# Sparse attention and MLP: x transposed by DMA for six batches, tokens taken in eight slices, outputs stored by partition halves

## The chip, the cores and the metric

The kernel runs on one core of a Trainium2 chip. The metric is the device time of one execution in microseconds (us); medians of several runs (slow ones among them) are given. For a program on one core a run counts as slow when it is over 1.5% above the fastest of the same kernel. A ratio is the mean time of one kernel's fast runs over that of the other's fast runs of the same rounds, so it is not quite the ratio of the medians quoted.

## The reference, cut to what matters

```python
B, H, S, D = 8, 8, 576, 64          # q, k, v: float32
mask_local   = (rel >= 0) & (rel < 32)                       # heads 0 to 3
mask_strided = (rel >= 0) & (pos % 32 == pos.T % 32)         # heads 4 to 7
attn = softmax(where(mask, q @ k.T / 8, -1e9)) @ v
x = attn.transpose(0, 2, 1, 3).reshape(4608, 512)            # tokens x channels
h = x @ w_in                                                 # 512 -> 2048
out = (h * tanh(softplus(h))) @ w_out                        # 2048 -> 512
```

Channels 0 to 255 of x come from the local heads, 256 to 511 from the strided heads.

## The kernel before: what the change and the argument touch

The MLP works in nine blocks of 512 tokens, numbered 0 to 8. In each block the first product fills `psh`, ScalarE applies the activation into `gT`, and the second product fills `pso`. The attention of batch t+1 is woven in between the matmuls of block t's second product. It leaves x with tokens on the partitions (`x_s[n, j]` holds token 8n+j of the strided heads), and TensorE transposes it into `xT`, a ring of four batches, with channels on the partitions:

```python
xT = const.tile([128, 4, RT], BF16, name="xT")          # RT = 4 * 576 tokens
...
def xt(self, kind, hf, eng=None):                       # kind "s": strided heads
    for j in range(CS):                                 # CS = 8
        nc.tensor.transpose(tr[:, PN*j:PN*j+PN], x_s[0:PN, j, 128*hf:128*hf+128], ident[0:PN, 0:PN])
    cast(eng, xT[:, 2 + hf, t0:t0 + S].rearrange("p (n j) -> p n j", j=CS), ...)   # ScalarE
```

The first product reads a contiguous piece of the ring, and the second product's result goes out by one large store for each 256 tokens:

```python
for a, n, o in segs(t):                                 # two pieces only where the ring ends: block 4
    for cc in (2, 3, 0, 1):
        nc.tensor.matmul(ps[:, u, o:o+n], lhsT=w_in[:, cc, ...], rhs=xT[:, cc, a:a+n], ...)
...
nc.scalar.copy(osb[:], p[:])
nc.sync.dma_start(out[r:r + 256, :].rearrange("(o p) d -> p o d", o=2), osb[:])
```

The sync engine (SP) issues its transfers in program order, each after its own wait. In block t that order is: transposes of the local q and k of batch t+1, loads of the local k and q of batch t+2, loads of v of batch t+2, the first store, transposes of the strided k and q of batch t+2, the second store. GpSimd's own queue loads the strided q and k.

The softmax here doesn't subtract the row's maximum and nothing guards it: scores larger than these inputs give would overflow.

## Time and profile before

| | before |
|---|---|
| median of 6 runs | 321.73 us (320.5 to 323.48) |
| span of the profiled run | 319.1 us |
| TensorE busy | 94% |
| a block of full attention and MLP (blocks 2, 3, 5, 6) | 32.48 us |
| TensorE's wait for `qTl` in block 1 | 1.4 us |

TensorE is the bound (94% busy), and the DMA row of the page stands at nine tenths or more for most of the first two thirds. The lines are in the prediction. A table by blocks, which the comparison will need, comes from cutting the span at the starts of the blocks' first products; the columns are the stretch, its length, the busy time of TensorE's matmuls, TensorE's weight loads, VectorE, ScalarE and GpSimd (each with its count of instructions), TensorE's granted clock as a share of full speed, the DMA share (the time of all packets over the time of the 16 engines; packets overlap, so it can pass 1) and GB/s. Of the kernel before, blocks 1 to 4:

```profile
63.83:97.88 34.05, 32.56 (x270) 16.10 (x269) 12.19 (x38) 19.80 (x23) 8.03 (x10) 1.00 1.22 199
97.88:130.36 32.48, 32.37 (x270) 16.06 (x268) 15.86 (x43) 19.75 (x22) 1.41 (x2) 1.00 1.18 202
130.36:162.84 32.48, 32.37 (x270) 16.04 (x269) 15.77 (x43) 19.74 (x22) 2.75 (x3) 1.00 1.17 175
162.84:195.48 32.64, 32.53 (x334) 22.32 (x332) 15.90 (x43) 19.75 (x22) 1.91 (x2) 1.00 1.07 168
```

Blocks 2 to 4 are full of TensorE work at full clock (granted 1.00; in block 1 TensorE waits 1.4 us), so 32.48 us is what a block costs when nothing else gets in the way.

### The profile page before, as it was taken

Reading aid. Unit: us, or ns where it says so; the run is one execution under the profiler, and the core shown is the slowest. Engines: PE = TensorE matmul, PEld = TensorE weight load, DVE = VectorE, ACT = ScalarE, POOL = GpSimd, SP = SyncE. Lnnn points to the kernel's source line nnn. Section 1 sums busy time; section 2 is a strip of 40 time slices with the busy share of each in tenths; the row PEclk is TensorE's granted clock in tenths of the full one; section 3 lists DMA queues with packets and bytes.
Section 4 is the critical chain, followed back from the end, with each engine's and each line's share of the span. In section 5 each row is a group of like instructions: output and inputs, shape, how many; then the busy total and the mean of one; then the engine's idle time right before and its main releaser. Section 6 shows DMA issues by size and latency. Waiting matters only on the chain.

```text
span 319.1 us, 5867 instructions
## 1 busy us (share of the span) xinstructions
PE 300.1 (94%) x2488; PEld 159.3 (50%) x2488; DVE 127.9 (40%) x332; ACT 172.6 (54%) x195; POOL 41.4 (13%) x50
## 2 busy tenths in 40 slices
PE   0678999999899999999999999999999999999995
PEld 0564455544454445444578555445544554444444
DVE  7672168600577047703870388028802820000000
ACT  2574563476437573767375746664666466315601
POOL 9288030145000100200020000000000000000000
PEclk9999999999999999999999999999999999999999
DMA  6999999999999999999979995898340100011011
GB/s 172 213 235 206 220 212 191 177 221 212 181 184 211 175 192 221 179 153 178 211 160 165 188 208 109 155 191 144 109 83 0 68 32 36 0 66 66 2 59 73
DMA packets 103114, 46.72 MB, mean 146 GB/s; under 512 B 85168, under 2 KB 95728, under 8 KB 103088
## 3 DMA queue, kind: packets, MB, share of 16 engines
q1 hardware_dynamic: 91648, 37.22, 64.6%
q0 software_dynamic: 11152, 8.92, 18.6%
q8 instruction: 19, 0.31, 0.4%
q10 hardware_dynamic: 288, 0.21, 0.2%
q14 instruction: 7, 0.06, 0.1%
HBM read 38.34 MB, written 9.44 MB: 150 GB/s over the span
## 4 chain that ended last, share of the span: by engine, by line
PE 81%; DVE 11%; DMA 4%; ACT 1%; issue 1%; SPq 0%; ACTq 0%
PE psh L428 38%; PE pso L467 28%; PE po L305 4%; PE pso L449 4%; DMA qTl<-ql 3%; PE ps L278 3%; DVE x_l L317 3%; DVE x_s L317 2%; PE trx L344 2%; DVE Pl L289 1%; DVE ks L151 1%; DVE rden L316 1%; DMA st<-in_k_dram 1%; PE trx L354 1%; PE tr L207 1%
## 5 line engine op out<-in xcount | busy, mean ns | idle before, releaser
L428 PE MATMUL psh<-xT,w_in 128*128 128x512 bf16 (+1 forms) x640 | 127.3, 360 | 0.0
L467 PE MATMUL pso<-w_out,gT 128*128 128x512 bf16 x512 | 126.3, 379 | 0.0
L433 ACT ACTIVATE gT<-psh 128x1024 bf16<-128x1024 f32 x72 | 73.6, 1023 | 44.0 <-PE psh L428 43.4
L428 PEld LDWEIGHTS <-w_in 128*128 128x128 bf16 x640 | 62.7, 98 | 62.2 <-issue 1.3
L467 PEld LDWEIGHTS <-gT 128*128 128x128 bf16 x512 | 43.6, 97 | 39.0
L289 DVE TENSOR_TENSOR Ps<-Ps,consts_sb 72x864 bf16<-72x864 bf16 (+1 forms) x24 | 13.2, 551 | 88.8 <-ACT Ps L283 88.8
L149 ACT COPY xT<-trx 128x576 bf16<-128x576 bf16 x32 | 20.1, 639 | 37.7 <-PE trx L354 28.2
L474 ACT COPY osb<-pso 128x1024 f32<-128x1024 f32 x16 | 16.2, 1012 | 22.6 <-PE pso L467 13.8
L283 ACT ACTIVATE Ps<-ps 72x864 bf16<-72x864 f32 (+1 forms) x24 | 18.5, 803 | 14.8 <-PE ps L278 14.8
L316 DVE RECIPROCAL rden<-po 72x4 f32<-72x4 f32 (+1 forms) x100 | 17.4, 174 | 18.8 <-PE po L305 18.6
L317 DVE TENSOR_TENSOR x_s<-po,rden 72x256 bf16<-72x256 f32 x56 | 23.5, 420 | 1.9
L151 DVE COPY osb<-pso 128x512 f32<-128x512 f32 (+1 forms) x2 | 1.1, 558 | 54.5 <-PE pso L449 54.5
L283 ACT ACTIVATE Pl<-ps 128x960 bf16<-128x960 f32 (+1 forms) x24 | 18.7, 806 | 3.6 <-PE ps L278 3.5
L305 PEld LDWEIGHTS <-Ps 72*128 72x128 bf16 x256 | 13.9, 101 | 12.5 <-DVE Ps L289 2.3
L317 DVE TENSOR_TENSOR x_l<-po,rden 96x256 bf16<-96x256 f32 x44 | 18.5, 420 | 1.5
L305 PE MATMUL po<-vs,Ps 72*128 72x65 bf16 x256 | 17.6, 201 | 0.9 <-DVE x_s L331 0.5
L97 POOL DMA_DIRECT2D ks<-in_k_dram x7 | 5.9, 842 | 80.7 <-DMA kTs<-ks 80.7
L305 PE MATMUL po<-vl,Pl 128*128 128x65 bf16 x192 | 12.9, 201 | 2.2 <-DVE x_s L317 0.7
L449 PE MATMUL pso<-w_out,gT 128*128 128x512 bf16 (+1 forms) x80 | 14.0, 336 | 0.0
L305 PEld LDWEIGHTS <-Pl 128*128 128x128 bf16 x192 | 9.9, 103 | 6.4 <-DVE x_l L317 1.8
L289 DVE TENSOR_TENSOR Pl<-Pl,consts_sb 128x960 bf16<-128x960 bf16 (+1 forms) x24 | 13.1, 545 | 0.0
L151 DVE CAST vl<-vl 128x768 bf16<-128x768 f32 x12 | 10.9, 942 | 0.8 <-DMA vl<-in_v_dram 0.8
(70 smaller groups left out, 178.0 us busy)
## 6 DMA issues: line engine op xcount, KB each, us to landing
out_dram<-osb SPq DMA_DIRECT2D x16, 512.0 KB, 3.6
vl<-in_v_dram SPq DMA_DIRECT2D x7, 768.0 KB
vs<-in_v_dram SPq DMA_DIRECT2D x8, 576.0 KB
kl<-in_k_dram SPq DMA_DIRECT2D x7, 576.0 KB, 8.7
ql<-in_q_dram SPq DMA_DIRECT2D x7, 576.0 KB, 9.4
w_out<-in_moe_w_out_dram POOLq DMA_DIRECT2D x4, 512.0 KB, 15.2
ks<-in_k_dram POOLq DMA_DIRECT2D x7, 288.0 KB, 8.0
qs<-in_q_dram POOLq DMA_DIRECT2D x7, 288.0 KB, 9.4
```

What stands on the lines that cost most here:

```text
L149: nc.scalar.copy(out_, in_)
L151: eng.tensor_copy(out_, in_)
L283: nc.scalar.activation(pt[0:n, :, 0:nw], ps[0:n, :, o0:o0 + nw], AF.Exp, scale=scale)
L289: meng.tensor_tensor(out=pm, in0=pm, in1=mk[0:n, :].unsqueeze(1).unsqueeze(1).to_broadcast([n, 2, nu, w]), op=ALU.mult,)
L305: nc.tensor.matmul(po[:, h, :], lhsT=pt[0:n, c0:c0 + 128], rhs=rhs, start=True, stop=True,)
L316: nc.vector.reciprocal(rden[0:m, :], po[0:m, :, D])
L317: nc.vector.tensor_tensor(out=dst.rearrange("p (h d) -> p h d", h=4), in0=po[0:m, :, 0:D], in1=rden[0:m, :].unsqueeze(2).to_broadcast([m, ...
L428: nc.tensor.matmul(ps[:, u, o:o + n], lhsT=w_in[:, cc, fc * 128:(fc + 1) * 128], rhs=xT[:, cc, a:a + n], start=(cc == 2), stop=(cc == 1),)
L433: nc.scalar.activation(gT[:, 2 * g:2 * g + 2, :], ps[:], AF.Mish)
L449: nc.tensor.matmul(p, lhsT=gT[:, fc, 128 * ot:128 * ot + 128], rhs=w_out[:, fc, c0:c1], start=(fc == 0), stop=(fc == 15),)
L467: nc.tensor.matmul(p[:, ot % 2, :], lhsT=gT[:, fc, 128 * ot:128 * ot + 128], rhs=w_out[:, fc, :], start=(fc == 0), stop=(fc == 15),)
L474: nc.scalar.copy(osb[:], p[:])
```

## The change

The intent is to take the strided transposes off TensorE. For batches 2 to 7 two DMA transposes per batch bring `x_s` straight into `xT_s`. A DMA transpose gives columns ordered by (j, n), so the tokens of a block are now taken as 8 slices of 64; both halves of `xT` are laid out so, with 80 columns per batch (72 used). A block crosses a batch boundary nearly always, so the first product is split in two in blocks 1 to 7. The rows of the second product come out as (parity of j, n) on the partitions, so each store becomes two DMAs of 64 partitions. The spare rows of `x_s` that the DMA transpose reads are cleared once. The local channels go first in the first product, the steps of the woven attention are reordered, and the last block's stores go mostly through ScalarE's queue in place of the sync queue.

```diff
-    xT = const.tile([128, 4, RT], BF16, name="xT")
+    xT_l = const.tile([128, 2, CS, RP], BF16, name="xT_l")
+    xT_s = const.tile([128, CS, 2, RP], BF16, name="xT_s")
...
+        def xt_dma(self, half):
+            c0, j0 = (self.b % RING) * SU, 4 * half
+            nc.sync.dma_start_transpose(
+                xT_s[:, j0:j0 + 4, :, c0:c0 + SU].rearrange("c j h n -> c (j h) n"),
+                x_s[0:SU, j0:j0 + 4, :].rearrange("p j x -> p (j x)"),
+            )
...  (steps of a batch: XD(0) after the fourth strided product, XD(1) after the eighth)
-        a, e, o, r = 512 * t, 512 * t + 512, 0, []
+        a, e, o, r = 64 * t, 64 * t + 64, 0, []
         while a < e:
-            n = min(e - a, RT - a % RT)
+            n = min(e - a, PN - a % PN)
...
+        ccs_all = (2, 3, 0, 1) if t < 2 else (0, 1, 2, 3)
...
+    def store(eng, t, ot, osb, c0=0, c1=DM):
+        rows = out[512 * t:512 * t + 512, :].rearrange("(p o i) d -> i p o d", o=4, i=2)
+        n = osb.shape[1]
+        for i in range(2):
+            eng.dma_start(rows[i, :, ot:ot + n, c0:c1], osb[64 * i:64 * i + 64])
...
+        Po.memset(x_s[64:SU], 0.0)
```

More of the change, by code (lines that the diff above doesn't have):

```diff
@@ L46 @@
     NBLK = NT // 512
-    RT = RING * S
+    RP = RING * SU
     consts_h = nc.inline_tensor(_consts(), name="consts")
@@ L338, in xt @@
             tr = tile_t("trx")[:].bitcast(BF16)
-            t0 = (self.b % RING) * S
+            c0 = (self.b % RING) * SU
             if kind == "l":
@@ L348, in xt @@
                 cast(
-                    eng, xT[:, 0:2, t0 + 288 * hf:t0 + 288 * hf + 288],
-                    tr[:, 0:576].rearrange("p (c n) -> p c n", c=2),
+                    eng, xT_l[:, :, :, c0 + 36 * hf:c0 + 36 * hf + 36],
+                    tr[:, 0:576].rearrange("p (c n j) -> p c j n", c=2, j=CS),
                 )
@@ L358, in xt @@
                 cast(
-                    eng, xT[:, 2 + hf, t0:t0 + S].rearrange("p (n j) -> p n j", j=CS),
-                    tr[:, 0:576].rearrange("p (j n) -> p n j", j=CS),
-                )
+                    eng, xT_s[:, :, hf, c0:c0 + PN],
+                    tr[:, 0:576].rearrange("p (j n) -> p j n", j=CS),
+                )
+        def xt_dma(self, half):
[4 more added lines that the diff above has]
+            )
     def attn_steps(b, x, y):
@@ L369, in attn_steps @@
         X = lambda kd, hf: (lambda: a.xt(kd, hf))
+        XD = lambda half: (lambda: a.xt_dma(half))
         s0, s1, sl2, l0, l1 = ("s", 0), ("s", 1), (("s", 2), ("l", 2)), ("l", 0), ("l", 1)
@@ L393, in attn_steps @@
             [Q(x, *sl2), Q(y, l0), V("s", 2)],
-            [V("s", 3), M("s", 2), M("l", 2)],
-            [V("s", 4), M(*l0)],
-            [Q(x, l1), V("s", 5)],
-            [V("s", 6), V("l", 5)],
-            [V("s", 7), M(*l1)],
-            [V("l", 0), V("l", 1)],
-            [X("s", 0), V("l", 2)],
-            [X("s", 1), V("l", 3)],
-            [V("l", 4), X("l", 0)],
+            [V("s", 3), XD(0), M("s", 2), V("s", 4)],
+            [V("s", 5), M("l", 2), M(*l0)],
+            [V("s", 6), V("s", 7), XD(1), Q(x, l1)],
+            [V("l", 5)],
+            [V("l", 0), M(*l1)],
+            [V("l", 1)],
+            [V("l", 2)],
+            [X("l", 0), V("l", 3)],
+            [V("l", 4)],
             [X("l", 1)], [],
@@ L407, in segs, with x_of @@
     def segs(t):
-        a, e, o, r = 512 * t, 512 * t + 512, 0, []
+        a, e, o, r = 64 * t, 64 * t + 64, 0, []
         while a < e:
-            n = min(e - a, RT - a % RT)
-            r.append((a % RT, n, o))
+            n = min(e - a, PN - a % PN)
+            r.append((a // PN % RING * SU + a % PN, n, o))
             a, o = a + n, o + n
         return r
+    def x_of(cc, a, n):
+        return xT_l[:, cc, :, a:a + n] if cc < 2 else xT_s[:, :, cc - 2, a:a + n]
     def mlp1(t, accs):
@@ L418, in mlp1, with group @@
         held = {}
-        def group(g, ccs=(2, 3, 0, 1)):
+        ccs_all = (2, 3, 0, 1) if t < 2 else (0, 1, 2, 3)
+        def group(g, ccs=ccs_all):
             if g not in held:
@@ L428, in group @@
                         nc.tensor.matmul(
-                            ps[:, u, o:o + n], lhsT=w_in[:, cc, fc * 128:(fc + 1) * 128],
-                            rhs=xT[:, cc, a:a + n], start=(cc == 2), stop=(cc == 1),
+                            ps[:, u, :].rearrange("p (j n) -> p j n", j=CS)[:, :, o:o + n],
+                            lhsT=w_in[:, cc, fc * 128:(fc + 1) * 128], rhs=x_of(cc, a, n),
+                            start=(cc == ccs_all[0]), stop=(cc == ccs_all[-1]),
                         )
-            if ccs[-1] == 1:
+            if ccs[-1] == ccs_all[-1]:
                 nc.scalar.activation(gT[:, 2 * g:2 * g + 2, :], ps[:], AF.Mish)
@@ L452, in part @@
                 )
-            r = 512 * t + 128 * ot
             osb = o_pool.tile([128, 2, DM], F32, tag="osb", name="osb")[:, 0, 0:c1 - c0]
             cast(nc.vector if n % 2 else nc.scalar, osb, p)
-            (nc.scalar if n == 3 else nc.sync).dma_start(out[r:r + 128, c0:c1], osb)
+            store(nc.sync if n == 4 else nc.scalar, t, ot, osb.unsqueeze(1), c0, c1)
         return [lambda n=n: part(n) for n in range(5)]
@@ L470, in group @@
                 )
-            r = 512 * t + 256 * (ot // 2)
             if g4 == 3 and ot % 2 == 1:
@@ L474, in group @@
                 nc.scalar.copy(osb[:], p[:])
-                nc.sync.dma_start(out[r:r + 256, :].rearrange("(o p) d -> p o d", o=2), osb[:])
+                store(nc.sync, t, 2 * (ot // 2), osb[:])
         order = [(ot, g4) for ot in range(4) for g4 in range(4)]
```

## The prediction

> **What bounds the kernel now.** I read the page first (busy shares, slices, chain), then the chain in order of time, then each engine's timeline in one block and in the start, then the sync queue's timeline.
>
> ```profile
> span 319.1 us, 5867 instructions
> ...
> PE 300.1 (94%) x2488; PEld 159.3 (50%) x2488; DVE 127.9 (40%) x332; ACT 172.6 (54%) x195; POOL 41.4 (13%) x50
> ...
> PE   0678999999899999999999999999999999999995
> ...
> DMA  6999999999999999999979995898340100011011
> ...
> PE psh L428 38%; PE pso L467 28%; PE po L305 4%; PE pso L449 4%; DMA qTl<-ql 3%; PE ps L278 3%; DVE x_l L317 3%; DVE x_s L317 2%; PE trx L344 2%; DVE Pl L289 1%; DVE ks L151 1%; DVE rden L316 1%; DMA st<-in_k_dram 1%; PE trx L354 1%; PE tr L207 1%
> ```
>
> TensorE is the bound from about 26 us on. The reader should also see the DMA row: nine tenths or more for most of the first 65% of the span. The one early wait for a transfer is `qTl` in the chain.[...]
>
> The chain in order of time gives the prices of the first MLP product, unsplit and split in two:
>
> ```profile
> 130.52 13.81 PE psh L428 x64
> ...
> 163.00 13.97 PE psh L428 x128
> ```
>
> 64 matmuls of 512 columns take 13.81 us, 215.8 ns each. The one block whose tokens cross the end of the ring has 128 of 256 columns in 13.97 us: splitting costs 0.16 us for 64 more matmuls, 2.5 ns each.
>
> TensorE's timeline in the second MLP product, where the attention of the next batch is woven in:
>
> ```profile
> 124.05 0.42 PE L305 MATMUL po<-vl,Pl 128*128 128x65 bf16 x8
> 124.31 1.02 PE L467 MATMUL pso<-w_out,gT 128*128 128x512 bf16 x4
> 125.19 0.43 PE L354 MATMUL trx<-consts_sb,x_s 72*128 72x72 bf16 x8
> 125.73 0.30 PE L305 MATMUL po<-vl,Pl 128*128 128x65 bf16 x4
> 125.87 1.02 PE L467 MATMUL pso<-w_out,gT 128*128 128x512 bf16 x4
> 126.73 0.42 PE L354 MATMUL trx<-consts_sb,x_s 72*128 72x72 bf16 x8
> 126.99 0.30 PE L305 MATMUL po<-vl,Pl 128*128 128x65 bf16 x4
> ```
>
> Start to start: the two groups of strided transposes take 0.54 us (125.19 to 125.73, of which about 0.28 is a wait, the evictions of the two small PSUM buffers being late) and 0.26 us (126.73 to 126.99), together 0.80 us per batch. Eight 65-column matmuls, each with its own weights, take 0.26 us, 32.5 ns each: a load of 128 weight columns fits under a matmul of about 32 ns.
>
> [...] in the start, the ks casts beside GpSimd memsets take 2270 ns, the equally large qs casts without them 676 ns.
> - [...] the packets of `vl`, the store and `kTs` near 98 us follow the order of issue.
>
> **The change part by part.**
>
> Removed: for batches 2 to 7, 16 transposes each on TensorE and two ScalarE copies of 639 ns. ScalarE is 54% busy, so the copies are worth nothing themselves. TensorE: 6 x 0.80 = 4.8 us. The order of steps is changed too: more of the strided products come early (steps 5 to 7). VectorE has about 0.55 us per product plus masks of 0.35 to 0.6 us in the same three steps: roughly 4.1 us of VectorE against 3.6 of TensorE. With two small PSUM buffers I count some 0.2 us of new waits per batch. Net gain 6 x 0.6 = **-3.6 us**.
>
> Added on TensorE: the token slices now split at every batch boundary instead of at the ring's end. Blocks 1 to 7 are split as 8+56, 16+48, 24+40, 32+32 and the mirror images (times 8 columns); only block 4 was split before. So 6 x 64 = 384 more matmuls (640 to 1024). [...] Four other blocks 0.16 each. Sum **+1.3 us**.
>
> Added in the start: a memset of 16x2048 on GpSimd, straight behind the two that now end at 8.56 us.
>
> ```profile
> 4.47 1.80 POOL L534 MEMSET ks<- 16x2048 bf16 x1
> 6.21 2.35 POOL L534 MEMSET qs<- 16x2048 bf16 x1
> 14.92 0.49 POOL L535 COPY held<-vs 1x4 bf16<-1x4 bf16 x1 [6.37 <-DVE vs L151]
> ```
> ```profile
> 4.64 4.46 DVE L151 CAST ks<-st 72x1024 bf16<-72x1024 f32 x2 [0.95 <-DMA st<-in_k_dram]
> 9.03 1.27 DVE L151 CAST qs<-st 72x1024 bf16<-72x1024 f32 x2
> ```
>
> GpSimd has 6.4 us free there, but [...] 2270 - 676 = 1.6 us later. That cast is on the starting path (transposes, scores, masks, values, all computing until 26 us; the weight loads hang on the vs cast behind it). **+1.6 us**.
>
> Added on the DMA side: two transposes of 80x1024 per batch, 640 packets of 256 bytes each. Two existing transposes of 1280 go through in about 1.3 to 1.8 us each when unhindered, so I reckon 0.9 us each, 1.8 us in a block of 32.5 us. [...] The stores by halves move the same 2 KB rows; twice as many issues, about 0.4 us of the sync queue each.
>
> When do the new transposes land? The queue is in order, and in block 1 it is far behind:
>
> ```profile
> 85.83 3.30 SPq L115 DMA_DIRECT2D vs<-in_v_dram  x1
> 89.23 0.40 SPq L129 DMA_DIRECT2D vl<-in_v_dram  x1
> 89.72 7.37 SPq L475 DMA_DIRECT2D out_dram<-osb  x1
> 97.19 2.59 SPq L172 DMA_TRANSPOSE kTs<-ks  x1
> ```
>
> The store was stuck 7.37 us in its issue, [...]; their packets end near 98 us, the store's near 100, and `kTs`, third in line, landed at about 103.2 us (GpSimd's wait for it ended then). The second x transpose takes that third place, with half the packets but the first x transpose ahead of it: landing near 102.5 to 103. The MLP of block 2 begins at 97.9 and reaches the strided channels after about 0.5 us (local channels come first now, which is what the new order is for). TensorE would wait there about **+4.5 us** (I take 2 to 6), once: after it the block runs that much later against the DMA. In block 2 the loads end near 124.7 against a need at 131; with 3.4 us more on the DMA side and 5.5 on TensorE's I get a margin near 3 us, then growing, as the queue idles from 178.5 to 186.9 in block 4.
>
> End: the last store is two issues of about 0.35 us on one queue instead of one: **+0.3 us**. ScalarE's own issues fit between its copies.
>
> Sum: -3.6 + 1.3 + 1.6 + 4.5 + 0.3 = +4.1 us, so 325.7 from 321.6. I shade this to **324.5 us**, since the two large additions (memset and first landing) are inferences, and any error in them goes mostly down.
>
> **The rivals.**
> - *The transposes are hidden everywhere.* For: the author put the strided channels last, and the later blocks have margins over 5 us. Against: block 1's store stuck 7.37 us. Then 321.2 us, and 319.6 if the memset is hidden too.
> - *DMA becomes the bound of blocks 1 to 4.* For: the DMA row, and half-width stores and transposes may be slower than I reckon. Against: the queue idles 4 us before the store of block 2 and 6.5 in block 3. Two to five us more per block would give 328 to 335.
> - *The strided moving operand streams slower.* For: never seen here. 5% of the first product's 124 us is 6 us: about 330.
> - *The clock drops after a long wait.* After the thin start, the first four matmuls at 26.5 us took 427 ns each before 216.[...]
> - *TensorE gains its whole share.* 6 x 0.80 is all there is, less 1.3 for splits: 318. Nothing in the profile gives 2%.
>
> **Range and chances.** The best case I can build is 318; the sum is 325.7; a DMA or streaming surprise reaches 330. So 318.5 to 330 for 8 in 10. Two per cent is 315.2 and 328.0. Faster 0.04, same 0.76, slower 0.20.
>
> **What would show each step.** Removal: TensorE's second MLP stretch falls from 18.67 (111.85 to 130.52) to about 18.1 us. Splits: 1024 matmuls at the first product; block 1's stretch at 14.2 us, others 13.97. Strided streaming is wrong if the unsplit blocks 0 and 8 leave 13.81 us. Memset: a qs cast over 2 us, `psh` beginning 1.6 us later. Landing: a wait of TensorE for a DMA into `xT_s` near 98 us, in block 2 alone; waits there in blocks 3 to 7 would mean that DMA is the bound, none at all that I misread the queue. End: the time from the last matmul to the end grows by 0.3 us.

## The result, and the profile after

The changed kernel takes 340.17 us (median of 6 runs, 337.94 to 341.86) against 321.73: ratio 1.0572, 95% interval 1.0516 to 1.0628. The prediction was 324.5, range 318.5 to 330. It was wrong: the change costs 18.4 us, and the prediction had 2.8.

The page of the changed kernel, the lines that answer to those shown of before:

```profile
span 339.3 us, 6472 instructions
...
PE 303.5 (89%) x2744; PEld 182.0 (54%) x2776; DVE 128.8 (38%) x332; ACT 165.1 (49%) x183; POOL 41.9 (12%) x51
...
PE   0578998999197899999996999999999999999995
...
PEclk9999999999879799999996999999999999999999
DMA  6999999999999999899999999899991052022023
```

TensorE's row has holes now, and under three of them the granted clock falls. The blocks, cut in the same way (blocks 1 to 4):

```profile
66.94:107.84 40.90, 33.95 (x313) 18.64 (x316) 11.96 (x37) 18.54 (x21) 8.03 (x10) 0.92 1.23 177
107.84:144.81 36.97, 33.50 (x314) 20.10 (x317) 15.67 (x43) 18.48 (x20) 1.41 (x2) 0.95 1.08 173
144.81:176.87 32.06, 31.66 (x314) 20.95 (x317) 15.66 (x43) 18.48 (x20) 1.41 (x2) 1.00 1.24 165
176.87:215.46 38.59, 34.46 (x314) 23.18 (x317) 15.65 (x43) 18.48 (x20) 1.41 (x2) 0.91 1.16 173
```

An undisturbed block (block 3; 5 and 6 are the same) is 32.06 us, 0.42 less than before: the change does gain what it was made for. Three blocks lose more than all gains together, and these three have a mean clock of 0.91 to 0.95. The whole difference of the two spans, block by block, is:

| stretch | before | after | difference |
|---|---|---|---|
| start, to the first `psh` | 26.49 | 28.00 | +1.51 |
| block 0 | 37.34 | 38.94 | +1.60 |
| block 1 | 34.05 | 40.90 | +6.85 |
| block 2 | 32.48 | 36.97 | +4.49 |
| block 3 | 32.48 | 32.06 | -0.42 |
| block 4 | 32.64 | 38.59 | +5.95 |
| blocks 5 and 6 | 64.96 | 64.12 | -0.84 |
| block 7 (no attention) | 27.63 | 27.79 | +0.16 |
| block 8 and the end | 31.03 | 31.9 | +0.9 |
| sum | 319.1 | 339.3 | +20.2 |

What TensorE waited for, from the list of waits (total, times, longest, in us), first of the kernel before, then of the changed one:

```profile
PE ps L278 <- DMA qTl<-ql: 1.4, 1, 1.4
```
```profile
PE psh L444 <- DMA xT_s<-x_s: 6.8, 2, 3.7
PE ps L279 <- DMA qTl<-ql: 6.6, 1, 6.6
```

The `xT_s` waits are at the beginning of blocks 2 and 4, the one for `qTl`, the transposed local q of batch 2, in block 1. TensorE's timeline at the first of them:

```profile
108.07 0.49 PE L444 MATMUL psh<-xT_l,w_in 128*128 128x384 bf16 x2
111.63 0.70 PE L444 MATMUL psh<-xT_s,w_in 128*128 128x384 bf16 x2 [3.07 <-DMA xT_s<-x_s]
```

And the sync queue ahead of it (start, time in the issue, both in us):

```profile
93.04 3.36 SPq L116 DMA_DIRECT2D vs<-in_v_dram  x1
96.50 0.43 SPq L130 DMA_DIRECT2D vl<-in_v_dram  x1
97.03 7.93 SPq L367 DMA_TRANSPOSE xT_s<-x_s  x1
105.05 1.29 SPq L462 DMA_DIRECT2D out_dram<-osb  x2
106.43 2.17 SPq L367 DMA_TRANSPOSE xT_s<-x_s  x1
```

The first x transpose sits in its issue for 7.93 us behind the loads of v for the batch after next, which nobody reads before the next block; the second goes behind the store, and its issue begins only 1.4 us before block 2 does (107.84).

### The profile page after: what moved, and what is told of

The parts are those of the page before. It is cut to its first block, busy times and chain, and to the rows that moved or that the text cites. A ratio compares the mean times of both kernels' runs of the same rounds, so it can differ in the third digit from the quotient of the medians.

```text
span 339.3 us, 6472 instructions
## 1 busy us (share of the span) xinstructions
PE 303.5 (89%) x2744; PEld 182.0 (54%) x2776; DVE 128.8 (38%) x332; ACT 165.1 (49%) x183; POOL 41.9 (12%) x51
## 4 chain that ended last, share of the span: by engine, by line
PE 78%; DMA 9%; DVE 8%; issue 2%; ACT 1%; SPq 0%; ACTq 0%
PE psh L444 38%; PE pso L490 27%; PE po L306 4%; DMA qTl<-ql 4%; DMA xT_s<-x_s 3%; PE pso L473 3%; PE ps L279 3%; DVE x_s L318 2%; PE trx L345 1%; DVE ks L152 1%; DMA st<-in_k_dram 1%; DVE Ps L290 1%; DVE rden L317 1%; DMA out_dram<-osb 1%; PE tr L208 1%
## 5 line engine op out<-in xcount | busy, mean ns | idle before, releaser
L490 PE MATMUL pso<-w_out,gT 128*128 128x512 bf16 x481 | 122.6, 383 | 1.2 <-issue 0.3
L444 PEld LDWEIGHTS <-w_in 128*128 128x128 bf16 x1024 | 86.9, 101 | 53.2 <-issue 11.8
L444 PE MATMUL psh<-xT_s,w_in 128*128 128x320 bf16 (+7 forms) x512 | 103.5, 296 | 6.8 <-DMA xT_s<-x_s 6.8
L444 PE MATMUL psh<-xT_l,w_in 128*128 128x320 bf16 (+7 forms) x512 | 102.8, 294 | 0.0
L450 ACT ACTIVATE gT<-psh 128x1024 bf16<-128x1024 f32 x72 | 73.6, 1024 | 57.9 <-PE psh L444 57.3
L150 ACT COPY xT_l<-trx 128x576 bf16<-128x576 bf16 x16 | 10.0, 640 | 36.0 <-PE trx L345 36.0
L306 PEld LDWEIGHTS <-Ps 72*128 72x128 bf16 x256 | 13.5, 104 | 13.0 <-DVE x_s L318 3.4
L284 ACT ACTIVATE Pl<-ps 128x960 bf16<-128x960 f32 (+1 forms) x24 | 18.7, 806 | 3.6 <-PE ps L279 2.9
L306 PE MATMUL po<-vs,Ps 72*128 72x65 bf16 x256 | 16.9, 204 | 2.3 <-DVE vs L152 1.1
L98 POOL DMA_DIRECT2D ks<-in_k_dram x7 | 5.0, 719 | 97.9 <-DMA kTs<-ks 97.9
L306 PEld LDWEIGHTS <-Pl 128*128 128x128 bf16 x192 | 11.4, 103 | 9.5 <-DVE x_s L318 2.4
L306 PE MATMUL po<-vl,Pl 128*128 128x65 bf16 x192 | 13.8, 201 | 1.6 <-DVE x_s L318 0.7
L279 PE MATMUL ps<-qTl,kTl 64*128 64x96 bf16 x192 | 8.2, 216 | 7.2 <-DMA qTl<-ql 6.6
```

The lines of the kernel that those rows point to most:

```text
L150: nc.scalar.copy(out_, in_)
L279: nc.tensor.matmul(ps[:, e, o:o + w], lhsT=lhsT, rhs=rhs, start=True, stop=True)
L284: nc.scalar.activation(pt[0:n, :, 0:nw], ps[0:n, :, o0:o0 + nw], AF.Exp, scale=scale)
L306: nc.tensor.matmul(po[:, h, :], lhsT=pt[0:n, c0:c0 + 128], rhs=rhs, start=True, stop=True,)
L444: nc.tensor.matmul(ps[:, u, :].rearrange("p (j n) -> p j n", j=CS)[:, :, o:o + n], lhsT=w_in[:, cc, fc * 128:(fc + 1) * 128], rhs=x_of(cc, ...
L450: nc.scalar.activation(gT[:, 2 * g:2 * g + 2, :], ps[:], AF.Mish)
```

## The experiments

Each run is told with its edit and what was written before it ran. Times are medians; the kernel before ran in the same rounds and had 321.3 to 322.4 us there. The changed kernel was not run again beside them, so a difference to its 340.17 us is one between rounds.

**Is the early part steady?** The control: the kernel before once more, as a run of its own (no edit).

> The kernel before, unchanged, as a control of the early part, since in the run with the halves alone the first product of the second block began 4.5 us later than before although no store had been issued yet. If the early part is steady from run to run, it times within 0.5% of before, the second block's first product begins at 63.8 us and the wait for qTl is near 1.4 us. If the early part is loose, the profile shows other waits in the first 65 us.

Measured: 321.71 us, ratio 1.0006. The second block's first product began at 65.26 us, 1.43 later than before, and the wait for `qTl` was 0.6. What made it later is not shown; an estimate comes from the two profiles above. In both the first product begins with 512-column matmuls of 427 ns each and goes on with 216: from 28.5 us in the kernel before, 2.0 after the first `psh`, and from 33.3 in the changed kernel, 5.3 after it. Half of these 3.3 us is lost, and block 0 is 1.60 longer there. The control's 1.43 would be 2.9 us more at 427 ns. So block 0 of single profiles differs by about 1.5 us, and the totals still agree within noise.

**The stores by halves.** First, the halves taken out of the changed kernel. ScalarE brings the hidden layer back to token order as it writes it, so the rows come out in order and the stores are whole, with the lines of before:

```diff
-nc.scalar.activation(gT[:, 2*g:2*g+2, :], ps[:], AF.Mish)
+nc.scalar.activation(gT[:, 2*g:2*g+2, :].rearrange("p u (n j) -> p u j n", j=CS),
+                     ps[:].rearrange("p u (j n) -> p u j n", j=CS), AF.Mish)
-store(nc.sync, t, 2 * (ot // 2), osb[:])
+nc.sync.dma_start(out[r:r + 256, :].rearrange("(o p) d -> p o d", o=2), osb[:])
```

> The changed kernel with ScalarE writing the hidden layer back in token order, so that the stores are whole again (one DMA of 128 partitions, queues as before); all else as changed. Theory H (the half-width stores delay the sync queue and so bring on the wait for qTl in block 1, 6.6 us, and part of the waits for xT_s): that wait falls under 2 us, the slow-clock stretch after it goes, and the time falls by 8 to 12 us to about 328 to 332. Theory X (the x transposes themselves are the load): the wait for qTl stays near 6 us, since it comes before the first x transpose, and the time stays within 2 us of 340.

Measured: 550.46 us. This told nothing of the stores: ScalarE itself became the bound. Its row of the costly groups (busy us, mean ns of one):

```profile
L450 ACT ACTIVATE gT<-psh 128x1024 bf16<-128x1024 f32 x72 | 328.7, 5002 | 4.5 <-PE psh L444 4.4
```

Here, for 128x1024, writing bf16 to SBUF in steps of eight elements costs 5002 ns, against 1024 in a row (the changed kernel). The same reordering with the loops the other way round (both sides `"p u n j"`, so that it reads PSUM in steps of 64 and writes in a row):

> The changed kernel with whole stores, the hidden layer brought back to token order by ScalarE in the other loop order: it now reads PSUM with a stride and writes in a row (the run that wrote with a stride took 5.0 us per activation). I expect 1.0 us per activation again. Theory H: qTl wait under 3 us, time 330 to 334. Theory X: 338 to 341.

Measured: 1024 ns per activation again, and 333.89 us, 6.3 less than the changed kernel (ratio to before 1.039, 1.0289 to 1.049, in place of 1.0572). The wait for `qTl` fell from 6.6 to 2.0 us, as theory H said; what is left are the waits for `xT_s`.

Then the halves alone in the kernel before:

```diff
-nc.sync.dma_start(rows, osb[:])
+for i in range(2):
+    nc.sync.dma_start(rows[64 * i:64 * i + 64], osb[64 * i:64 * i + 64])
```

> The kernel before with nothing but its 16 large stores cut into two halves of 64 partitions, same rows. Theory H: the sync queue comes 1.5 to 2 us later to the local transposes of batch 2, the wait for qTl grows from 1.4 to 3 to 6 us, and the time rises to 324 to 330. Theory X: no more than 322.5, within noise of before.

Measured: 327.63 us, ratio 1.0167. But this profile had 4.5 of its us in block 0, ahead of the first store, so the kernel ran again:

> The kernel before with stores cut by partition halves, a second time, with more rounds. In its first profile 4.5 us of the loss stood in block 0, ahead of the first store, which the halves cannot have caused. If the loss belongs to the halves, the time is again 325 to 329 and this profile shows where from the first store on. If part of it was a loose early phase, the time falls to 322 to 325.

Measured: 328.22 us, ratio 1.0158 (1.0106 to 1.0211). Now block 0 was as in the control, and the loss stood in block 1, where TensorE waited for `qTl`:

```profile
PE ps L278 <- DMA qTl<-ql: 6.2, 1, 6.2
```

So the halves cost about 6 us by themselves, both times (5.1 to 5.4 by the ratios, whose intervals exclude 1). In the odd block 0 of the first profile VectorE waits 2.4 us for a load of v, TensorE for VectorE (up to 1.95 us), and matmuls at half rate follow (four of 512 columns in 1.69 us in place of 0.86); why the load was late in that run is not shown. Is it the halved width or the doubled count? The kernel before, stores cut in two along the other axis, 128 partitions each:

> The kernel before with its 16 large stores cut in two again, but each half with all 128 partitions (128 rows of 2 KB). Theory H1 (half the partitions is what slows a store: 2 KB packets of 158 to 184 ns in the first half of an undisturbed store, against 84): the packets stay near 84 ns and the time within 1% of before, well under the 327.6 of the halves. Theory H2 (twice the DMA instructions on the sync queue are what costs): 326 to 328, as the halves by partition.

Measured: 321.51 us, ratio 1.0005: it is the width. From the summaries of the stores, first of this run, then of the one with halves (issue time min/median/max in ns; landing in us):

```profile
L477 SPq DMA_DIRECT2D out_dram<-osb x32: 332/424/7007, 66.9 to 292.1; - x32
...
DMA to landing us min/median/max: 2.2/3.3/5.2
```
```profile
L477 SPq DMA_DIRECT2D out_dram<-osb x32: 595/601/4491, 67.6 to 297.0; - x32
...
DMA to landing us min/median/max: 3.1/4.3/5.2
```

In the packet records of undisturbed late stores, 512 KB take 1.43 us from first start to last end with full width (kernel before, 84 ns per packet of 2 KB) and 2.18 us by halves (changed kernel, 159 ns in the first half of the packets, 90 in the second).

A store that is 0.75 us longer does not make 6 us. What does, is what comes next in the queue: the local transposes of batch 2, beside which GpSimd's four loads run. Here they are held back until the transposes have landed, with half stores in the kernel before:

```diff
+if t == 1:
+    Po.tensor_copy(held[:], qTl[0:1, 1, 0:4])
 for b in range(max(3, t + 2 + (t > 1)), min(t + 4, B)):
     load_qk_str(b)
```

> The kernel before with half stores, and GpSimd's four loads of block 1 held back until the local transposes of batch 2 have landed. Theory Q (half stores cost 6 us because they push those transposes under the four loads): no wait for qTl over 2 us, no slow clock after it, 321.5 to 323.5. Rival (the half stores' own slowness is the delay): the wait stays at 4 us or more and the time at 326 to 329.

Measured: 324.32 us, ratio 1.0039 (0.9995 to 1.0084). The wait in block 1 is gone (block 1 takes 32.5 us) and two thirds of the cost with it. In the profiled run, the slowest of the six, 5.5 us came back in block 2: two waits for `qTl` of 1.2 and 1.0 us, then 6 us at half clock (four 512-column matmuls in 1.71 us; the page's PEclk stands at 7 in two slices). Theory Q holds for the larger part. The transposes show it directly: the last one of `qTl` has landed 2.7 us after its issue began (77.96 to 80.65), and beside the four loads it took 9.7 us in the kernel before (75.02 to 84.7) and 13.5 with half stores (77.03 to 90.5). The same in the changed kernel, with half stores and x transposes in:

> The changed kernel, where GpSimd first reads one element of qTl and so issues its four loads of batches 3 and 4 in block 1 only after the local transposes of batch 2 have landed. Theory Q (these four loads, 1152 packets of 1 KB beside the transposes, are what holds the transposes back): the wait for qTl goes from 6.6 us to under 1, the 6.8 us at half clock after it goes too, the time falls by 7 to 10 us to 330 to 333. Rival (the transposes are late by the queue ahead of them): the wait stays above 4 us.

Measured: 339.22 us, no gain, against my expectation of 330 to 333 (the profiled run was a slow one). The wait for `qTl` went, and the waits for `xT_s` took its place:

```profile
PE psh L444 <- DMA xT_s<-x_s: 14.8, 4, 7.4
```

GpSimd's loads came later. That what stood behind them came later for this reason, and that a delay taken out at one wait returns at the next, is how I read it; a single slow profile does not show it.

**The memset.** The changed kernel with the memset on VectorE, behind its own memsets and ahead of its first cast:

```diff
+Dv.memset(x_s[64:SU], 0.0)
-Po.memset(x_s[64:SU], 0.0)
```

> The changed kernel with the new memset on VectorE, in its idle time before the first cast, in place of GpSimd. Theory M (the memset holds up a cast of the start[...]): the qs casts take 1.3 us again, the first product begins at 26.5 us, and at least 1.5, at most 3.5 us go; if the later waits for qTl and xT_s hang on this shift, more. Rival (the shift is caught up by the waits for DMA later): under 1 us, since the later waits end with a DMA anyway.

Measured: 337.2 us, 3.0 less, but the intervals of the two ratios overlap (1.0429 to 1.0581 here, 1.0516 to 1.0628 for the changed kernel). In the profile the start gives back 1.53 us and block 1 2.9, as the wait for `qTl` falls from 6.6 to 3.4; so not all of the 3.0 is the memset's own. And the memset alone, on GpSimd, in the kernel before:

> The kernel before with the memset of x's spare rows added on GpSimd in the start, nothing else. Theory M: the qs casts take 3.0 us together in place of 1.3, the first product begins 1.5 us later, and 1.5 to 2 us stay to the end: 323 to 324[...]. Rival: the wait for loads in blocks 0 and 1 takes it up: 321.5.

Measured: 323.73 us, ratio 1.0059 (1.0009 to 1.0108), the first product at 28.00 us as predicted. VectorE and GpSimd in the start of the changed kernel:

```profile
9.03 2.96 DVE L152 CAST qs<-st 72x1024 bf16<-72x1024 f32 x2
```
```profile
8.51 2.34 POOL L557 MEMSET x_s<- 16x2048 bf16 x1
```

The two casts took 1.27 us before, with no memset beside them. Now the first takes 2.37, from 9.03 to 11.40, with the memset beside it until 10.85, and the second 0.67.

**The x transposes.** The changed kernel with TensorE transposing every batch, in the order of before; slices, half stores and memset stay:

```diff
-[V("s", 3), XD(0), M("s", 2), V("s", 4)], ... [V("s", 6), V("s", 7), XD(1), Q(x, l1)], ...
+[V("s", 3), M("s", 2), M("l", 2)], ... [X("s", 0), V("l", 2)], [X("s", 1), V("l", 3)], ...
-ccs_all = (2, 3, 0, 1) if t < 2 else (0, 1, 2, 3)
+ccs_all = (2, 3, 0, 1)
```

> The changed kernel with the strided x of every batch transposed on TensorE again (step order and channel order of before); layout by slices, split matmuls, half stores and the memset stay. Theory X: the two waits for xT_s (6.8 us) and the slow clock after them (about 5 us) go, 6 x 0.42 us of TensorE work comes back: about 331 to 333, with the wait for qTl in block 1 still there at about 6 us. Theory H: as much is left as the stores cost, so over 330; if it falls to 326 or less, the qTl wait too came from the x transposes.

Measured: 331.22 us, 9 less; the wait for `qTl` is still there (8.7 us in the profiled run, a slow one). So the parts stand side by side: the x transposes with all their gains, and with the orders of steps and channels that came with them, cost 9 us, the rest of the change 10.

The opposite: the transposes as pure extra DMA work in the kernel before, into a tile that nobody reads, TensorE still transposing.

```diff
+xd = const.tile([128, CS, 2, SU], BF16, name="xd")
-[V("s", 3), M("s", 2), M("l", 2)],       ... [V("s", 7), M(*l1)],
+[V("s", 3), XD(0), M("s", 2), M("l", 2)], ... [V("s", 7), XD(1), M(*l1)],
```

> The kernel before with the twelve DMA transposes of x added at the same places in the sync queue, into a tile that nothing reads; TensorE still transposes x itself; the memset of the spare rows is on VectorE. Theory X1 (what costs is that the in-order queue is later for all that stands behind it: loads, local transposes): waits for qTl or loads grow and the time rises to 325 or more. Theory X2 (what costs is only that TensorE waits for the transposes themselves, which stand behind the loads of the next batch): within 1% of before, 320.5 to 324.

Measured: 321.8 us, ratio 1.0013. The extra 1.97 MB and twelve instructions cost nothing that can be seen (0.9961 to 1.0065). What costs is that TensorE waits for them. With whole stores and the memset on VectorE, only this is left of the change:

> The changed kernel with whole stores and the memset on VectorE: only the slices, the split matmuls and the x transposes are left of the change. If the two parts add up (6.3 and 3.0): 330.5 to 332, with waits for xT_s in blocks 2 and 4 of 4 to 6 us each left and slow clock after both.

Measured: 331.32 us (329.21 to 331.4). Additive as expected. The profiled run, the fastest, shows one wait for `xT_s`, 4.4 us at the beginning of block 2, and slow matmuls after it (122 of the first product take 16.16 us, where 128 take 13.97 in a split block that waits for nothing); in block 4 it had none, so that one comes and goes from run to run.

Now the same with the loads of v behind the x transposes in the queue (and so also behind the first store and the strided k and q):

```diff
-if t + 2 < B:
+if t + 2 < B and t == 0:
     load_v(t + 2)
...
 at[9].append(lambda: transpose_str(t + 2))
+at[9].append(lambda: load_v(t + 2))
```

> As the run before it in this list, but the loads of v for two batches on are issued behind the second x transpose of a block in place of ahead of the first: the same DMA work in another order. Theory X2 (place in the in-order queue): both waits for xT_s go, no slow clock, six blocks of 32.06 us: 318.5 to 320.5, the fastest of all. Theory X1 (DMA is simply full in the early blocks): the waits come back at other tiles, v or qTl, and the time stays over 325.

Measured: 320.29 us, ratio to before 0.9945 (0.9911 to 0.9978); the waits for `xT_s` are gone, the clock stays up (mean granted clock 1.0 in the profiled run). The x transposes in block 1's queue, where block 2 begins at 98.85:

```profile
88.62 5.16 SPq L367 DMA_TRANSPOSE xT_s<-x_s  x1
94.49 1.43 SPq L367 DMA_TRANSPOSE xT_s<-x_s  x1
```

In the run before it the second was issued from 101.31 to 102.81, with block 2 beginning at 100.91. VectorE's casts now wait up to 6.8 us for v, and nothing waits for VectorE there. Theory X2 holds: 11 us hung on what stands ahead of two transposes in one queue. With half stores and GpSimd's memset left in:

> The changed kernel with half stores and the memset on GpSimd as changed, and only the loads of v moved behind the second x transpose. Theory A (half stores hurt only where TensorE waits for what stands behind them in the queue, which the new order takes away except in block 1): 320.3 of the last run plus 1.9 for the memset and up to 2: 322 to 325. Theory B (half stores cost their 6 us through the wait for qTl in block 1, before the new order acts): 327 to 332, with a wait for qTl over 3 us.

Measured: 329.67 us (327.08 to 331.5 and a slow run of 333.86), with 5.7 us of waiting for `qTl`: theory B. The half stores strike in block 1 before the new order acts. And the new order alone in the kernel before:

> The kernel before with only the loads of v moved behind the strided transposes of the same block. If the gain of the fastest run so far (320.3) comes from the change itself (0.42 us in each of six blocks), this one stays at 321.5 to 322.5. If the order of the loads alone is worth it, this one is at 320.5 or less.

Measured: 322.15 us, ratio 1.0005. The order is worth nothing without the change. Finally the fastest version with GpSimd's loads held back as well, and that hold alone in the kernel before:

> The fastest version so far (whole stores, memset on VectorE, loads of v behind the x transposes: 320.3), with the same holding back of GpSimd's loads. If the 2.0 us wait for qTl in block 1 is due to those loads, 318.3 to 319.3; if the loads then come too late for the transposes behind them, no gain or a loss of 1 to 3 us.

> The kernel before, whole stores, with only GpSimd's four loads of block 1 held back. Its wait for qTl in block 1 is 1.4 us, so at most that can be gained: 320.5 to 322. If it is at 318.5 or less, the fastest version owes its time to this and not to the change.

Measured: 318.31 us, ratio 0.9878 (0.9849 to 0.9906), and for the hold alone 320.5 us, ratio 0.9986 (0.9937 to 1.0035). So x transposes by DMA are worth about 1% with whole stores, the memset on VectorE and both queues in order. The page of the fastest version:

```profile
span 316.8 us, 6428 instructions
...
PE 295.7 (93%) x2744; PEld 178.5 (56%) x2776; DVE 128.9 (41%) x333; ACT 165.0 (52%) x183; POOL 40.0 (13%) x51
```

## Why the prediction was wrong, point by point

- *Removal (-3.6 us).* Right. The woven stretch fell from 18.67 to 18.09 us (block 3: 158.78 to 176.87), as predicted.
- *Splits (+1.3).* Right in kind, a little large: the split blocks that wait for nothing take 13.97 us for the first product, also those with 64-column pieces (blocks 1 and 7), for which I had 14.2 by an estimate of 0.35 us each. Six times 0.16 is 1.0. The 64-column matmuls, each with its own weight load, run at 29 ns from start to start.
- *Slow strided streaming (rival).* Wrong: the unsplit block 8 takes 13.81 us as before.
- *Memset (+1.6).* Right: 1.51 in the start, 1.8 alone. The estimate took the first qs cast beside the memset at 2270 ns, as the ks casts beside theirs, in place of 676; it took 2.37 us. In the changed kernel its removal was worth 3.0 with the wait behind it (intervals overlap). That the matmuls went from 427 to 216 ns only 5.3 us after the first `psh`, in place of 2.0, adds 1.6 in block 0 of this profile; the control, 1.43 late without a memset, shows that this part can be chance.
- *End (+0.3).* Too small: 0.9, of which the last stores by halves, taking 1.4 us in place of 0.8 by their packet records, are 0.6.
- *Stores by halves ("the same 2 KB rows; twice as many issues, about 0.4 us of the sync queue each").* **This step failed in kind.** It was sized at nearly nothing and measures 6 us (6.3 and 5.8 alone in the kernel before, 6.3 within the changed kernel). I priced the bytes and the issues, and not the width: an undisturbed store takes 2.18 us by halves and 1.43 whole, and two full-width pieces lose nothing (ratio 1.0005). Why the width matters is not shown. Then the delay grows: the local transposes of batch 2 fall under GpSimd's four loads, and TensorE waits.
- *Landing of the x transposes (+4.5 in block 2, a margin near 3 us after).* **This step failed in size.** The mechanism was right and was seen in the right block: position in the queue behind the loads of v. But it was sized at 4.5 and is worth 11.0 (331.32 less 320.29, by order alone). Two terms were mis-sized. The margin in block 3 was not there in the profiled run: TensorE waited 3.7 us at the beginning of block 4 too. (The working of that margin cannot be redone: 131 + 5.5 - 124.7 - 3.4 is 8.4, not 3.) And the clock after a long wait, which I had among the rivals with an estimate of 1 to 2 us, takes more: the granted clock stands at 0.50 for 3.4 us (111.8 to 115.2) from the end of the wait of 3.1 us, and for 6.8 us (91.3 to 98.1 and 180.0 to 186.9) from 2.0 and 1.4 us before the ends of those of 6.6 and 3.7. Half of what falls behind the wait is lost, 1.7 to 2.7 us each time. Four 512-column matmuls take 1.69 us there in place of 0.86.
- *The rival "DMA becomes the bound of blocks 1 to 4: 328 to 335"* came nearest in size, and the wait at block 4 is the sign I had named for it, but it fails in kind: the same DMA work in another order runs in 320.3 us, and unused transposes cost nothing. It was not the amount but the order.

The parts add up: 6.3 for the halves, 3.0 for the memset in the changed kernel, 9.4 for the x transposes as placed (331.32 less 321.93; this has the removal's gain of 3.5 and the splits in it) make 18.7, against 18.4 measured. By the ratios to the kernel before of the same rounds they are 5.9, 2.2 and 8.8, 16.9 together; so the sum holds to 2 us, not to 0.3. Open are why halves are slower, why a load of v was late in block 0 of one profile, why the wait before block 4 comes and goes, and why the clock stands at half for 6.8 us at two of the three waits and for 3.4 at the other.

## What to carry to other kernels

When work moves from an engine to a DMA queue, ask what stands ahead of it in that queue: a transfer that is needed at once does not belong behind a prefetch that is needed a block later (one sat 7.93 us in its issue here), and putting the prefetch behind it cost nothing here (ratio 1.0005 in the kernel before). Price a transfer by the partitions it spans, not by its bytes alone: the same 512 KB took 1.43 us over 128 partitions and 2.18 in two halves of 64. And a wait of several us on TensorE cost more than its length here, since the clock fell: at those of 3.1, 3.7 and 6.6 us in the changed kernel it stood at 0.50, and four 512-column matmuls took 1.69 us in place of 0.86 after those of 3.4 us (memset on VectorE) and 6.2 (halves again). For shorter ones no limit came out: matmuls as slow followed one of 2.2 us (the first run with the halves alone), one of 1.8 (whole stores and memset) and two of 1.2 and 1.0 us close together, but not one of 2.0 us (the run with the loads of v behind).
